# A fused attention and maxout FFN kernel: batch 0 split at query 240, and FFN block 0 in two token parts

## The chip, the cores and the metric

The kernel runs on one core of a Trainium2 chip. The core has five engines that each work through their own instructions in the order in which these were emitted: TensorE (PE in the profile, with PEld for its weight loads), VectorE (DVE), ScalarE (ACT), GpSimd (POOL) and SyncE (SP, which here only issues transfers). Transfers are issued from a queue on SP, ACT or POOL and run beside the engines. Only TensorE multiplies matrices, and its results land in PSUM, eight banks of 2 KB a partition, from where VectorE or ScalarE must fetch them.

The metric is the device time of one execution in microseconds (us), as a median over runs. A stamp such as 29.68 is a time from the start of the profiled span.

## The reference

Eight batches of eight-head attention with 16 "beacon" keys ahead of the 576 causal ones, and behind it, over all 4,608 tokens, an FFN that takes the maximum of three products and multiplies it once more:

```python
k_all = concatenate([beacon_k, k], axis=2)          # 16 + 576 keys
v_all = concatenate([beacon_v, v], axis=2)
scores = scale * q @ k_all.T                        # 8 batches, 8 heads, 576 queries, D = 64
scores = where(causal, -1e9, scores)                # beacon keys are seen by all queries
a = exp(scores - scores.max(-1))
a /= a.sum(-1) + 1e-9
x = (a @ v_all) as [4608 tokens, 512]               # token = batch * 576 + query
h = maximum(maximum(x @ w1, x @ w2), x @ w3)        # 768 columns
out = h @ w_out                                     # [4608, 512], fp32
```

## The kernel before, in words

**Quads.** The kernel goes through 16 "quads" Q = 2b + g: batch b, and four of its eight heads (g = 0 or 1). For each quad q and k lie transposed in SBUF (`qTs`, `kTs`, two buffers each, so quad Q takes the buffer of Q − 2). They come by a transfer, a cast to bf16 (done by an engine for quads 0 and 1, in the transfer itself for later ones, `load_qk16`), and four transposes on VectorE (`turn`, L180 to L188: k in two pieces, q in two).

**Scores in bursts.** Keys lie in five tiles t of up to 128; tile t is seen by the queries from `q_min[t]` = 0, 112, 240, 368, 496 on. The list `bursts` (L61) says which tiles with which queries are scored together; four bursts (c = 0 to 3) make a quad. `emit_scores` (L241) does the matmuls of a burst into two PSUM tiles `sc` of two heads each. There are only two such tiles, so a burst's scores wait for the exponentials of the burst before. For quads 0 and 1 the matmuls go two heads at a time, for the others four. `emit_exp(i)` (L267, ScalarE) turns one `sc` tile into `at_sb`; `emit_masks` (L284, GpSimd) sets to zero what lies beyond the diagonal.

**PV passes.** `pv_pass(Q, hf, part)` (L297) treats one half of the queries (hf = 0 or 1, 288 each). Part 0 multiplies `at_sb` with ones: the sums of the softmax, of which ScalarE makes reciprocals with a Ln and an Exp (L325, L327). Parts 1 and 2 multiply with V, and VectorE multiplies the result with the reciprocals into `xT` (L331), the transposed input of the FFN. PSUM has two tiles for these passes. `pv_pairs` puts the six passes of a quad in three pairs.

**The FFN.** Tokens go in nine blocks of 512. `mm1_unit(tb, ft, i)` makes 128 of the 768 columns of `x @ w_i` for one block: four matmuls of 512 tokens (two groups of 256 in block 4, where the ring of `xT` ends), and then a copy to `hT` for i = 0 (ScalarE, VectorE in block 0) or a maximum on VectorE for i = 1, 2. `mm2_unit` multiplies 128 tokens with `w_out`. A block is 18 + 4 = 22 units; PSUM has two tiles for them. Block 0 holds tokens of batch 0 alone, block 1 of batches 0 and 1, and so on.

**The order.** All is emitted by hand. `emit_all` (L493) goes through Q and c; a step emits a PV pair of the quad before, the burst's scores, one exponential, perhaps an FFN unit, the other exponential, the masks, and what `plan` holds for the step (loads, casts, transposes). FFN units are emitted up to a running limit `allowed`, which grows by `rate` a step, and only if the block's last batch is `ready`; `ready` goes to b − 1 at (4, 0) and then at step c = 3 of each even quad. Block 0 begins after quad 1's last PV pair, within step (2, 0), in an order by weights: six units of w1, then six of w2, six of w3. Rates are 22/11 = 2 units a step up to (4, 2) and 126/45 = 2.8 after it.

**Loads.** `begin` (L442) issues on SP's queue k and q of quads 0 and 1, the beacon keys of quad 1 (`load_first_beacon_k`), V of batch 0 in five tiles (`load_v`, cast to bf16 by VectorE), and the beacon keys of batch 1. POOL's queue then issues quad 2 at (0, 1), w1 at (0, 3), w2 at (1, 0), quad 3 at (1, 1), V of batch 1 from (1, 2) on, w3 at (2, 1), and w_out at (3, 0). In the text W0, W1 and W2 are the weights of i = 0, 1 and 2.

Of the kernel before, what the change touches and what calls it, by code (L numbers as in the profile page):

```python
# [16 lines left out]
def kernel(  # L17
# [43 lines left out]
    bursts = [  # L61
        [(0, 0, HALF), (3, q_min[3], S)],
        [(1, q_min[1], S)],
        [(2, q_min[2], S)],
        [(0, HALF, S), (4, q_min[4], S)],
    ]
    NC = len(bursts)
    at_piece = {}
    burst_at = []
    pos = 0  # L70
    for burst in bursts:
        start = pos
        for t, q0, q1 in burst:
            at_piece.setdefault(t, []).append((q0, q1, pos))
            pos += q1 - q0
        burst_at.append((start, pos))
    AT_W = pos
# [15 lines left out]
    nrm_pool = ctx.enter_context(tc.tile_pool(name="nrm", bufs=2))  # L93
    ffn_h = ctx.enter_context(tc.tile_pool(name="ffn_h", bufs=2))
# [97 lines left out]
    def load_v(b, queue=None):  # L192
        queue = queue or nc.sync
# [3 lines left out]
        for t in range(n_kt):  # L197
# [43 lines left out]
    def emit_scores(Q, c):  # L241
# [5 lines left out]
        a0, a1 = burst_at[c]  # L247

        for heads in ((0, 1), (2, 3)) if Q < n_quad else (range(HG),):
            off = 0  # L250
            for t, q0, q1 in bursts[c]:
# [24 lines left out]
    def emit_masks(Q, c):  # L276
        at_sb = at[Q]
        off = burst_at[c][0]
        for t, q0, q1 in bursts[c]:
# [17 lines left out]
    def pv_pass(Q, hf, part):  # L297
        b, g = divmod(Q, n_quad)
        at_sb, v_sb = at[Q], v_tiles[b]
        h0, h1 = hf * HALF, (hf + 1) * HALF  # L300
        runs = []
        for t in range(n_kt):
            for q0, q1, a in at_piece[t]:
# [3 lines left out]
        ps = pv_psum.tile([128, HALF], FP32, name="pv")  # L307
# [15 lines left out]
        if part == 0:  # L323
            lnd = nrm_pool.tile([128, HALF], FP32, name="lnd")
            nc.scalar.activation(out=lnd, in_=ps, func=AF.Ln)  # L325
            recip = nrm_pool.tile([128, HALF], FP32, name="recip")
            nc.scalar.activation(out=recip, in_=lnd, func=AF.Exp, scale=-1.0)  # L327
            recips[Q, hf] = recip
        else:
            c0 = b % RING * S + h0  # L330
            nc.vector.tensor_mul(xT[:, 2 * g + part - 1, c0 : c0 + HALF], ps, recips[Q, hf])  # L331
# [15 lines left out]
    def mm1_unit(tb, ft, i, pool, name):  # L347
# [15 lines left out]
        if i == 0 and tb > 0:  # L363
            nc.scalar.copy(hT[:, ft, :], ps)  # L364
        elif i == 0:

            nc.vector.tensor_copy(hT[:, ft, :], ps)
        else:
            nc.vector.tensor_max(hT[:, ft, :], hT[:, ft, :], ps)  # L369

# [35 lines left out]

    units = []
    for tb in range(n_tokb):
        last_b = (TOKB * (tb + 1) - 1) // S

        order = [(ft, i) for ft in range(n_ft) for i in range(3)]
        if tb == 0:
            order.sort(key=lambda x: x[1])
        for ft, i in order:
            units.append((last_b, mm1_unit, (tb, ft, i)))
# [15 lines left out]

    plan = {}
# [153 lines left out]
```

## Time and profile before

| | us |
|---|---|
| median of 3 runs | 295.66 (295.62 to 296.06) |
| profiled execution | 294.93 |
| its span, first to last instruction | 293.2 |
| TensorE busy in the span | 273.2 (93%) |
| ScalarE, VectorE, GpSimd busy | 159.2, 170.4, 87.9 |

The profile is one execution. A timeline row gives start, length, engine, line, operation, output and input, their shapes, a count of merged instructions (xN), and in brackets how long the engine stood idle before them and what released it. A row of the groups has busy time, mean ns of one, and idle time before. A busy TensorE is not TensorE at its full rate: the end of a matmul is modelled, and neighbours overlap.

### The profile page before, as it was taken

To read this page: it belongs to the slowest core of one execution; us is meant where nothing else is said; L and a number is where in the kernel's file an instruction comes from. 1 tells how busy PE (TensorE), PEld (TensorE's weight loads), DVE (VectorE), ACT (ScalarE), POOL (GpSimd) and SP (SyncE) were. 2 spreads that over 40 slices of the span, in tenths; PEclk is the share of its full clock that TensorE was granted. 3 is DMA by queue.
4 is the path that set the end of the run, shared out by engine and by line. 5 is a ranking of instruction groups with operands and counts; after the bars stand their busy time and mean duration, and the time that the engine had idled before them with its cause. 6 is when DMAs were issued, how large, how long until landed. Compare 5 with 4: busy or idle time off the path is not lost.

```text
span 293.2 us, 7619 instructions
## 1 busy us (share of the span) xinstructions
PE 273.2 (93%) x3208; PEld 137.1 (47%) x3246; DVE 170.4 (58%) x296; ACT 159.2 (54%) x246; POOL 87.9 (30%) x156
## 2 busy tenths in 40 slices
PE   0797999999999999999999999999989999999995
PEld 0245345434445444444548775544444445444442
DVE  3717769765656575647474656656653455555553
ACT  5798485468574655567645857465565742220210
POOL 0573953126231623134322623152212410000000
PEclk9999999999999999999999999999999999999999
DMA  7999999668147905491348506690038003003003
GB/s 251 231 183 206 121 187 185 111 188 147 36 83 202 189 2 81 144 218 35 49 141 186 101 2 116 192 167 2 23 133 155 2 2 132 14 0 134 13 0 143
DMA packets 51922, 33.05 MB, mean 113 GB/s; under 512 B 41264, under 2 KB 42288, under 8 KB 51888
## 3 DMA queue, kind: packets, MB, share of 16 engines
q1 hardware_dynamic: 41152, 20.40, 27.1%
q0 software_dynamic: 10464, 12.01, 26.0%
q8 instruction: 25, 0.41, 0.6%
q10 hardware_dynamic: 272, 0.15, 0.2%
q14 instruction: 9, 0.07, 0.1%
HBM read 35.13 MB, written 9.44 MB: 152 GB/s over the span
## 4 chain that ended last, share of the span: by engine, by line
PE 85%; ACT 7%; DVE 3%; issue 2%; DMA 1%; ACTq 0%; DVEq 0%
PE fps L356 41%; PE fps L376 14%; PE pv L315 12%; PE sc L256 10%; PE sc L356 5%; ACT at_sb L267 4%; DMA first<-in_beacon_k_dram 1%; PE sc L376 1%; DVE xT L331 1%; ACT lnd L325 1%; DVE qT L183 1%; DVE hT L369 1%; ACT recip L327 1%; ACT hT L364 1%; ACTq L141 0%
## 5 line engine op out<-in xcount | busy, mean ns | idle before, releaser
L356 PE MATMUL fps<-xT,w_sb 128*128 128x512 bf16 (+1 forms) x621 | 134.7, 355 | 2.8 <-issue 1.3
L267 ACT ACTIVATE at_sb<-sc 128x992 bf16<-128x992 f32 (+3 forms) x128 | 105.1, 860 | 55.0 <-PE sc L256 54.7
L369 DVE TENSOR_TENSOR hT<-hT,fps 128x512 bf16<-128x512 bf16 x96 | 65.8, 686 | 70.7 <-PE fps L356 62.4
L356 PEld LDWEIGHTS <-w_sb 128*128 128x128 bf16 x720 | 66.5, 98 | 72.0 <-issue 12.2
L284 POOL TENSOR_SCALAR_AFFINE_SELECT at_sb<-at_sb 128x512 bf16<-128x512 bf16 (+2 forms) x80 | 46.7, 593 | 135.5 <-ACT at_sb L267 128.3
L256 PE MATMUL sc<-qT,kT 32*128 32x288 bf16 (+4 forms) x768 | 43.1, 298 | 10.8 <-DVE qT L183 8.5
L364 ACT CAST hT<-fps 128x512 bf16<-128x512 f32 x42 | 24.6, 586 | 39.7 <-PE fps L356 39.7
L376 PE MATMUL fps<-w_out_sb,hT 128*128 128x512 bf16 x183 | 44.0, 379 | 0.7 <-issue 0.3
L331 DVE TENSOR_TENSOR xT<-pv,recip 128x288 bf16<-128x288 f32 x64 | 27.1, 450 | 10.8 <-PE pv L315 10.6
L384 DVE COPY y<-fps 128x512 f32<-128x512 f32 x32 | 22.1, 691 | 18.7 <-PE fps L376 14.9
L376 PEld LDWEIGHTS <-hT 128*128 128x128 bf16 x210 | 19.6, 97 | 26.4 <-issue 3.9
L256 PEld LDWEIGHTS <-kT 32*128 32x128 bf16 x768 | 17.4, 95 | 30.1 <-issue 16.2
L315 PE MATMUL pv<-at_sb,v_sb 128*32 128x288 bf16 (+4 forms) x1024 | 29.2, 255 | 1.7 <-DVE xT L331 1.6
L315 PEld LDWEIGHTS <-v_sb 128*32 128x32 bf16 (+1 forms) x1024 | 21.9, 96 | 15.4 <-issue 12.9
L183 DVE STREAM_TRANSPOSE kT<-c 128x256 uint32<-128x256 uint32 (+1 forms) x32 | 21.6, 705 | 3.6 <-ACT c L176 3.5
L183 DVE STREAM_TRANSPOSE qT<-c 128x256 uint32<-128x256 uint32 (+1 forms) x32 | 21.6, 705 | 0.0
L325 ACT ACTIVATE lnd<-pv 128x288 f32<-128x288 f32 x32 | 12.9, 402 | 13.8 <-PE pv L315 13.8
L356 PE MATMUL sc<-xT,w_sb 128*128 128x512 bf16 x70 | 18.2, 379 | 0.1
L209 POOL CAST v_sb<-vst 128x1024 bf16<-128x1024 f32 (+1 forms) x18 | 16.1, 893 | 6.8 <-DMA vst<-in_v_dram 6.8
L315 PE MATMUL pv<-at_sb,ones 128*32 128x288 bf16 (+4 forms) x512 | 15.2, 261 | 0.6 <-DVE xT L331 0.6
L327 ACT ACTIVATE recip<-lnd 128x288 f32<-128x288 f32 x32 | 14.2, 443 | 1.0
L315 PEld LDWEIGHTS <-ones 128*32 128x32 bf16 (+1 forms) x512 | 10.6, 97 | 8.2 <-issue 5.6
(35 smaller groups left out, 63.5 us busy)
## 6 DMA issues: line engine op xcount, KB each, us to landing
out_dram<-y SPq DMA_DIRECT2D x35, 256.0 KB, 2.0
vst<-in_v_dram SPq DMA_DIRECT2D x21, 256.0 KB, 4.7
c<-in_k_dram POOLq DMA_DIRECT2D x14, 288.0 KB, 4.4
c<-in_q_dram POOLq DMA_DIRECT2D x14, 288.0 KB, 5.2
w_sb<-in_moe_w_dram POOLq DMA_DIRECT2D x3, 768.0 KB, 9.2
vst<-in_v_dram SPq DMA_DIRECT2D x7, 224.0 KB, 3.5
vst<-in_v_dram SPq DMA_DIRECT2D x7, 160.0 KB, 5.3
w_out_sb<-in_moe_w_out_dram POOLq DMA_DIRECT2D x1, 768.0 KB, 11.2
```

What stands on the lines that cost most here:

```text
L183: nc.vector.transpose(dst.rearrange("p (t s) -> p s t", s=RUN)[:, s0:s1], src.rearrange("p (s d) -> p s d", d=DP),)
L256: nc.tensor.matmul(sc[h // 2][:, h % 2, off : off + w], kT[hs, 128 * t : 128 * (t + 1), j], qT[hs, q0:q1, j], start=(j == 0), stop=(j == 1 ...
L267: nc.scalar.activation(out=at_sb[:, 2 * i : 2 * i + 2, a0:a1], in_=sc[i][:, :, 0 : a1 - a0], func=AF.Exp, scale=scale,)
L284: nc.gpsimd.affine_select(out=view, in_=view, compare_op=ALU.is_ge, fill=0.0, base=q0 - (128 * t - Nb), pattern=[[0, HG], [1, edge - q0]], ...
L315: nc.tensor.matmul(ps[32 * j : 32 * j + 32, lo - h0 : hi - h0], lhsT, at_sb[0:n, j, a : a + hi - lo], start=(i == 0), stop=(i == len(runs) ...
L327: nc.scalar.activation(out=recip, in_=lnd, func=AF.Exp, scale=-1.0)
L331: nc.vector.tensor_mul(xT[:, 2 * g + part - 1, c0 : c0 + HALF], ps, recips[Q, hf])
L356: nc.tensor.matmul(ps[:, o0 : o0 + n], w_in[i][:, ct, 128 * ft : 128 * (ft + 1)], xT[:, ct, x0 : x0 + n], start=(ct == 0), stop=(ct == n_c ...
L364: nc.scalar.copy(hT[:, ft, :], ps)
L369: nc.vector.tensor_max(hT[:, ft, :], hT[:, ft, :], ps)
L376: nc.tensor.matmul(ps, hT[:, ft, 128 * tt : 128 * (tt + 1)], w_out_sb[:, ft, :], start=(ft == 0), stop=(ft == n_ft - 1),)
L384: nc.vector.tensor_copy(y, ps)
```

## The change

It does four things.

1. **Batch 0's queries are split at E = 240 instead of 288.** A class `Layout` now holds bursts and parts. Quads 0 and 1 use the layout `first`: its burst 0 holds all keys that queries 0 to 239 see, bursts 1 to 3 the rest (432 query columns each; burst 0 has 368). The other quads keep theirs.
2. **Order of batch 0** (`emit_first`, new): burst 0 and 1 of quad 0, burst 0 of quad 1, and then sums and products of the first parts of both quads, mixed with further bursts.
3. **FFN block 0 in two token parts, weight by weight** (`early_unit`, `block0`): for each w_i three units of two column tiles over tokens 0 to 239, then six units of one column tile over tokens 240 to 511; 27 units for 18, 144 matmuls for 72. For i = 0 VectorE copies the first part's results and ScalarE the second part's. Calls of `emit_block0` are put by hand between the bursts of quads 1 to 3. `emit_first` also holds all of quads 2 and 3 and of block 0. The loop of `emit_all` begins at quad 4, with `ready` = 1 and with 126/48 units a step.
4. **Loads**: the beacon keys of quad 1 go ahead of its q, those of batches 2 to 7 move into `begin`, SP loads only two tiles of batch 0's V and POOL the other three, W0 is issued before quad 2, and `load_w`, `load_quad`, `load_v16` stand in new places.

The PSUM tile of a PV pass becomes a full bank, and the reciprocals get a pool of four buffers.

```diff
+    E = q_min[2]
+    C1, C2 = E + 96, E + 192
+    first = Layout(
+        E,
+        [
+            [(1, q_min[1], E), (0, 0, E)],
+            [(0, E, S), (1, E, C1)],
+            [(1, C1, S), (2, E, C2)],
+            [(2, C2, S), (3, q_min[3], S), (4, q_min[4], S)],
+        ],
+    )
...
+    def layout(Q):
+        return first if Q < n_quad else usual
...
-        h0, h1 = hf * HALF, (hf + 1) * HALF
+        h0, h1 = layout(Q).parts[hf]
...
+    def early_unit(i, fts, x0, x1, copy):
+
+        if 0 not in hTs:
+            hTs[0] = ffn_h.tile([128, n_ft, TOKB], BF16, name="hT")
+        n = x1 - x0
+        bank = ffn_psum.tile([128, TOKB], FP32, name="fps")
+        ps = bank.rearrange("p (f n) -> p f n", f=len(fts))[:, :, 0:n]
+        for f, ft in enumerate(fts):
+            for ct in range(n_ct):
+                nc.tensor.matmul(
+                    ps[:, f],
+                    w_in[i][:, ct, 128 * ft : 128 * (ft + 1)],
+                    xT[:, ct, x0:x1],
+                    start=(ct == 0),
+                    stop=(ct == n_ct - 1),
+                )
+        hT = hTs[0][:, fts[0] : fts[-1] + 1, x0:x1]
+        if i == 0:
+            copy(hT, ps)
+        else:
+            nc.vector.tensor_max(hT, hT, ps)
...
+    block0 = []
+    for i in range(3):
+        for ft in range(0, n_ft, 2):
+            block0.append((early_unit, (i, (ft, ft + 1), 0, E, nc.vector.tensor_copy)))
+        for ft in range(n_ft):
+            block0.append((early_unit, (i, (ft,), E, TOKB, nc.scalar.copy)))
+    for tt in range(TOKB // 128):
+        block0.append((mm2_unit, (0, tt, ffn_psum, "fps")))
...
         load_qk(1, 1, (0, QS))
+        load_first_beacon_k(1, nc.sync)
         load_qk(1, 0, (0, QS))
-        load_first_beacon_k(1, nc.sync)
-        load_v(0)
+        load_v(0, 2)
         load_beacon_k(1, 2, nc.sync)
+        load_beacon_k(2, B, nc.sync)
...
+    def burst(Q, c, n=0):
+
+        emit_exp = emit_scores(Q, c)
+        emit_exp(0)
+        emit_block0(min(n, 1))
+        emit_exp(1)
+        emit_masks(Q, c)
+        emit_block0(max(n - 1, 0))
...
+        begin()
+        burst(0, 0)
+        load_w(0)
+        cast_v(0, 0, 2, by_dve)
+        burst(0, 1)
+        burst(1, 0)
+        load_v16(0, 2, 5)
+        sums(0, 0)
+        burst(0, 2)
+        load_quad(2)
+        sums(1, 0)
+        products(0, 0)
+        burst(0, 3)
+        load_w(1)
+        products(1, 0)
+        burst(1, 1, 2)
+        load_quad(3)
+        burst(1, 2, 1)
+        load_w(2)
+        sums(0, 1)
+        burst(1, 3)
+        turn_beacon_k(1, 2)
+        put_beacon_k(2, by_dve)
+        products(0, 1)
+        turn_all(2, 1)
+        turn_all(2, 0)
+        sums(1, 1)
+        burst(2, 0)
+        load_v16(1, 0, 2)
+        products(1, 1)
+        emit_block0(2)
+        burst(2, 1, 2)
+        load_v16(1, 2, 5)
+        burst(2, 2, 2)
+        put_beacon_k(3, by_pool)
+        load_w_out()
+        burst(2, 3)
+        load_quad(4)
+        for which in (1, 0):
+            emit_block0()
+            turn_all(3, which)
+        emit_block0()
+        turn_beacon_k(2, B)
+        burst(3, 0, 2)
+        emit_pv(pv_pairs(2)[0])
+        burst(3, 1, 2)
+        put_beacon_k(4, by_pool)
+        burst(3, 2, 2)
+        load_quad(5)
+        burst(3, 3, 2)
+        emit_block0(2)
+        emit_pv(pv_pairs(3)[0])
+        for Q in (2, 3):
+            for pair in pv_pairs(Q)[1:]:
+                emit_pv(pair)
+                emit_block0(min(2, len(block0) - 4))
+        turn_all(4, 1)
+        turn_all(4, 0)
+        while block0:
+            emit_block0()
...
-        early = range(n_quad * NC, (2 * n_quad + 1) * NC - 1)
-        early_rate = 22 / len(early)
-        rate = (len(units) - 3 * 22 - 6) / (NQ * NC - early.stop)
-        for Q in range(NQ):
+        rate = (len(units) - 2 * 22 - 6) / (NQ * NC - early_q * NC)
+        for Q in range(early_q, NQ):
```

More of the change, by code (lines that the diff above doesn't have):

```diff
@@ L277, in emit_masks @@
         at_sb = at[Q]
-        off = burst_at[c][0]
-        for t, q0, q1 in bursts[c]:
+        off = layout(Q).burst_at[c][0]
+        for t, q0, q1 in layout(Q).bursts[c]:
             edge = min(q1, 128 * t - Nb + k_rows[t])
```

166 lines of the change are left out of this document (78 added, 88 removed).

## The prediction

> **What bounds the kernel now.** I read the page first, then windows of engine busy time, then each engine's timeline over the first 60 us.
>
> ```profile
> span 293.2 us, 7619 instructions
> PE 273.2 (93%) x3208; PEld 137.1 (47%) x3246; DVE 170.4 (58%) x296; ACT 159.2 (54%) x246; POOL 87.9 (30%) x156
> PE   0797999999999999999999999999989999999995
> 8.00:28.00 20.00, 16.97 (x264) 8.19 (x264) 10.54 (x23) 16.70 (x25) 12.11 (x19) 1.00 1.07 205
> 36.00:44.00 8.00, 7.89 (x103) 3.65 (x108) 5.37 (x10) 6.18 (x10) 4.97 (x10) 1.00 1.12 185
> 44.00:52.00 8.00, 7.95 (x143) 4.14 (x140) 7.34 (x16) 4.61 (x9) 2.91 (x6) 1.00 1.05 175
> ```
>
> Each window row gives its stretch, its length, then busy us and instructions of PE, PEld, DVE, ACT and POOL, the granted clock, DMA share and GB/s. From 28 us on TensorE (PE) is full: 7.89 and 7.95 of 8 us. Whatever leaves it idle there is lost time. From 8 to 28 us ScalarE (ACT) sets the pace: 16.70 of 20. PE's 16.97 there are stretched matmuls, as the rows of the timelines show:
>
> ```profile
> 9.03 1.89 ACT L267 ACTIVATE at_sb<-sc 128x992 bf16<-128x992 f32 x2 [1.90 <-PE sc L256]
> 11.07 2.50 ACT L267 ACTIVATE at_sb<-sc 128x928 bf16<-128x928 f32 x3 [0.15 <-PE sc L256]
> 18.38 1.83 ACT L267 ACTIVATE at_sb<-sc 128x928 bf16<-128x928 f32 x2 [0.15 <-PE sc L256]
> 26.92 0.44 ACT L327 ACTIVATE recip<-lnd 128x288 f32<-128x288 f32 x1
> 21.35 0.92 PE L315 MATMUL pv<-at_sb,v_sb 128*32 128x288 bf16 x24
> 43.81 0.63 PE L315 MATMUL pv<-at_sb,v_sb 128*32 128x288 bf16 x24
> 46.71 1.18 PE L315 MATMUL pv<-at_sb,v_sb 128*32 128x288 bf16 x40
> 47.82 0.51 PE L256 MATMUL sc<-qT,kT 32*128 32x288 bf16 x16
> 40.63 0.90 PE L315 MATMUL pv<-at_sb,ones 128*32 128x288 bf16 x32
> 29.14 0.88 DVE L331 TENSOR_TENSOR xT<-pv,recip 128x288 bf16<-128x288 f32 x2 [0.48 <-PE pv L315]
> 29.68 1.67 PE L356 MATMUL fps<-xT,w_sb 128*128 128x512 bf16 x7 [0.16 <-issue]
> ```
>
> Exps follow each other with 0.15 us between them; batch 0's last reciprocal ends at 27.36 and the FFN starts at 29.68. The same 24 matmuls take 0.92 us at 21 us and 0.63 at 44: PE runs at about half speed until some 22 us, though the granted clock column says 1.00. So before 28 us PE has some 9 us of work, by its full-speed prices, in 20; it is this slack that the change can use.
>
> **The price list.** Exp, Ln, copy, multiply, transpose, mask and load:
>
> ```profile
> L267 ACT ACTIVATE at_sb<-sc 128x992 bf16<-128x992 f32 x10 | 9.4, 994 | 6.2 <-PE sc L256 6.1
> L267 ACT ACTIVATE at_sb<-sc 128x928 bf16<-128x928 f32 x10 | 9.0, 940 | 4.2 <-PE sc L256 4.2
> L267 ACT ACTIVATE at_sb<-sc 128x736 bf16<-128x736 f32 x8 | 5.9, 782 | 3.3 <-PE sc L256 3.2
> L267 ACT ACTIVATE at_sb<-sc 128x672 bf16<-128x672 f32 x8 | 5.5, 726 | 1.1 <-PE sc L256 1.1
> L325 ACT ACTIVATE lnd<-pv 128x288 f32<-128x288 f32 x8 | 3.2, 402 | 2.2 <-PE pv L315 2.2
> L364 ACT CAST hT<-fps 128x512 bf16<-128x512 f32 x8 | 4.7, 586 | 5.0 <-PE fps L356 5.0
> 34.35 1.24 DVE L183 STREAM_TRANSPOSE kT<-c 128x256 uint32<-128x256 uint32 x2
> 37.78 1.27 DVE L369 TENSOR_TENSOR hT<-hT,fps 128x512 bf16<-128x512 bf16 x2
> 29.47 1.17 POOL L284 TENSOR_SCALAR_AFFINE_SELECT at_sb<-at_sb 128x448 bf16<-128x448 bf16 x2 [3.94 <-ACT at_sb L267]
> 16.83 0.72 POOL L232 DMA_DIRECT2D w_sb<-in_moe_w_dram  x1
> w_sb<-in_moe_w_dram POOLq DMA_DIRECT2D x1, 768.0 KB, 8.3
> 24.20 0.84 POOL L225 DMA_DIRECT2D v_sb<-in_v_dram  x1
> 10.64 1.14 POOL L176 CAST c<-st 128x1152 bf16<-128x1152 f32 x1 [9.60 <-DMA st<-in_q_dram]
> 11.56 0.27 DVE L144 CAST first<-first 128x64 bf16<-128x64 f32 x1 [0.85 <-DMA first<-in_beacon_k_dram]
> 4.97 1.74 SPq L141 DMA_DIRECT2D first<-in_beacon_k_dram  x4
> ```
>
> Neighbours on ACT overlap by 0.1 us or so (two of 992 take 1.89), and a timeline row of PE includes 0.07 that overlaps with the next. The change's new widths lie between rows: a pair of exps of 864 (432 queries, two heads) costs 1.55, of 736 1.35 start to start; Ln and reciprocal together 0.6 for 240 queries, 0.75 for 336; an FFN copy of 272 columns 0.33; a max of 480 columns 0.6. Exp elements in all are unchanged (1,664 query columns per head either way). Half-speed scores of 432 queries take 0.74 per two heads, at full speed 0.42.
>
> **Halved FFN matmuls.** These rows stand for the split at 240:
>
> ```profile
> 129.57 2.84 PE L356 MATMUL fps<-xT,w_sb 128*128 128x512 bf16 x12
> 132.34 0.90 PE L315 MATMUL pv<-at_sb,ones 128*32 128x288 bf16 x32
> 160.91 2.86 PE L356 MATMUL fps<-xT,w_sb 128*128 128x256 bf16 x24
> 163.70 0.90 PE L315 MATMUL pv<-at_sb,ones 128*32 128x288 bf16 x32
> ```
>
> Three units as 12 matmuls of 512 take 132.34 − 129.57 = 2.77 us, as 24 of 256 take 2.79. So 72 more matmuls in block 0 cost 6 × 0.02 = 0.1 us. The sums and products of batch 0 get 24 more short matmuls (9 runs of four for 8, times 6 passes): the 24 matmuls of the 0.63 row are 0.023 apiece, columns included, so 24 more without more columns are 0 to 0.5 us; I take 0.2, since the columns are most of that price. Together **+0.3**. The Trainium skill (TensorEngine Tiling, Instruction Overhead) gives each matmul about 60 cycles of overhead. Added 72 times, at the 2.4 GHz of its page on TensorE, that would be 1.8 us, an estimate; the two pairs of rows don't agree with it, and they decide.
>
> **Batch 0, walked through ACT's order.** Stamps are sums of the rows above. Exps (0,0) 8.8 to 10.1, (0,1) 10.5 to 12.1. Next in order is now Q1's first burst. Its q is cast on POOL from 10.64 and turned on VectorE (DVE): 11.78 + 1.24 = 13.0. Before, DVE sat on the beacon rows until 11.56; the change issues those ahead, so this wait goes, but q1's own load goes four issues (1.74 us of SP) later. I take 13.4 (between 13.0 if its queue hides that, 14.7 if not). Half the scores at half speed: exps (1,0) 14.3 to 15.6. ACT idle 2.2, which Q0's own bursts filled before. Then (0,2) 16.2 to 17.7, Ln and reciprocal to 18.3. The second product of Q0 shares a PSUM buffer with Q1's sum, so it waits for that Ln, and (0,3)'s scores stand behind it: (0,3) 19.35 to 20.9, idle 1.05. (1,1) 21.45 to 23.0, idle 0.55. W0 is now the first load on POOL's queue, issued at 13.2; with 8.3 to landing it is there at 21.5, hidden by (1,1)'s scores until 22.0; each us later costs a us. Three tiles of V move from SP's queue (and two casts from DVE) to POOL's: 2.5 us of issues (three of 0.84) at 17 to 19.5, behind which stand the masks of (0,2) and (0,3), done at 22.3 and wanted at 25.3, and Q2's loads, issued at 20.1; hidden, with 3 us to spare for the masks. The tiles must land by 27. Two units of the first part (0.83 each) run 22.0 to 23.65, with (1,2)'s scores behind them: exps 24.3 to 25.85, idle 1.3. Third unit, sum (0,1), its reciprocal to 26.95, exps (1,3) to 28.5; batch 1's beacon rows (0.8 us of DVE) lie beside this. Two masks, 1.17: 29.7; only now do the last rounds of sum (1,1) run, and the reciprocal ends at 30.95 instead of 27.36. Meanwhile DVE, after the products of (0,1) at 28.85, turns Q2's k and q: two times 1.2, to 31.25. PE has scores (2,0) ahead of products (1,1): 31.35, products to 33.1, last multiply 33.75, first second-part unit **33.9**. The same walk over the kernel before ends at 30.0, where the row has 29.68.
>
> So 4.2 later, with three of 27 units done ahead (2.6 us of PE): **+1.6**.
>
> **Q2's and Q3's bursts.** Before, each step had some two whole units and a PV pair, over 3 us of PE beside 1.3 to 1.9 us of exp. Now a step of (2,1) to (2,2) has two half units: PE 0.5 + 2 × 0.47 = 1.4; ACT 1.65 (or 1.25) + two copies 0.66 = 2.3 (1.9), since W0's second-part copies go to ACT. Scores wait for the exps one burst back: PE idles 1.4 and 1.0. At (2,3) three first-part units of W1 (2.5 us of PE) alternate on DVE with Q3's turns: 0.6 + 1.2 + 0.6 + 1.2 = 3.6 us, and (3,0) needs the last turn: idle 2.2. Then Q2's four Ln and reciprocal instructions lie on ACT: (3,1) 0.35, (3,2) 1.6, (3,3) 0.6. Sum **+7.2**. Of the moved loads, W1 (issued about 22.3) and Q3 (23) get 8.3 us and more, and are due at 40: hidden by a margin of 6; uncovered, they cost us for us. Behind (3,3) all is FFN and PV; a product waiting for an Ln costs 0.4, and the four y copies stand behind Q4's turns (2.4 us): 1.1. **+1.5**. Changes between kinds of matmul, 0.16 us in the row of 29.68, cost nothing where PE waits anyway; four or five fall into these gaps: **−0.7**.
>
> **The steps after.** Q4 now starts with block 0 done, with 22 units of block 1 allowed at 126/48 = 2.625 a step. Block 2 becomes ready only at (6,3), 11 steps later: 28.9 allowed, 22 there. (6,1) and (6,2) go without FFN: PE has 0.83 + 0.42, then 0.56 + 0.31; ACT has a pair each of 1.76, 1.65, 1.25 and four Ln/reciprocal, 1.3. Idle 2.2. Block 2 runs out again before (8,3) (49.9 allowed, 44 there): 2.2. Before, the same point had 46.4 allowed for 44, less than one step without FFN, and PE is at 9 there on the page's line. **+4.4**. Opening block 1 stalls now thus:
>
> ```profile
> 62.47 0.59 ACT hT L364
> 63.06 0.64 ACT at_sb L267
> ```
>
> 1.3 us and a mode change, against 0.9 by the same sum at (4,1): **−0.5**.
>
> **Sum.** 0.3 + 1.6 + 7.2 + 1.5 − 0.7 + 4.4 − 0.5 = 13.8. The profiled execution took 294.93 (span 293.2 and 1.7 around it), 0.7 below the median of 295.66: 294.9 + 13.8 = **308.7 us**.
>
> **Rivals.** (1) *Faster*: three units really come out of idle time. If products (1,1) end by 32.3 (29.7 + 2.6) and the half units keep PE above 9.5 of 10 us through Q3, the start gains 2.6 and the opening stall 0.5, less 0.3: 292.1. For it speaks that PE has some 11 us to spare before 28 us; against it that 24 of 27 units need the second part anyway, and that exps and their masks stand between. 7%. (2) *The change does little of what it says*: three units of 27 move, (1) gains its 2.6, one starved stretch (2.2) takes it back, 294.5 to 296: 4%. (3) *Only the start and Q2/Q3 cost*, no starved steps: 304.3; for it, the catching-up steps could run ahead; against it, block 2 cannot start before (6,3). 17%. (4) *Loads or a slow PE*: W0 or Q2 late by 3 to 4 us, or half speed until 24 us (+1.5): 312 to 314; before, a load of Q3's k issued at 20.9 behind W1 took 9.4:
>
> ```profile
> c<-in_k_dram POOLq DMA_DIRECT2D x1, 288.0 KB, 9.4
> ```
>
> Against it, W0 has the queue to itself. 9%. (5) *PE falls back to half speed* in the thin stretch 34 to 53: its 13.7 us of work there would be 27.4 in 21 us, 6.5 more: 315. The rows show no fall-back after 23 us, but no such gaps either. 3%. The Trainium skill (TensorE: Matmul & The Clock Gate, Part 1) puts the fall-back behind an idle window of some 3.4 us; by that rule, with gaps of at most 2.2, (5) doesn't come.
>
> **How the numbers follow.** The forecast as summed has 60%, 306 to 311.
>
> Faster by over 0.2% (about what a measurement can tell) 0.07, within 0.04, slower 0.89. Range: 301 to 313, which leaves out (1), (2), (5) and half of (4), 18%; it takes in q1's two ends (13.0 to 14.7), the halved matmuls' and 2 us on each of the large terms.
>
> **What would show it.** The first FFN matmul at 22, the first of 272 columns at 34; ACT idle about 2 us near 12 to 14; PE near 6 of 10 from 34 to 53, with scores waiting for exps and once for a transpose of Q3; PE gaps near Q6 and Q8 with no FFN matmul between scores. PE dense from 22 us on would prove it wrong, above all a first 272-column matmul before 32.

## The result and the profile after

The changed kernel takes 320.26 us as a median of 4 runs (318.00 to 321.54), the kernel before 295.64 beside it (4 runs): a ratio of 1.083, 95% interval 1.076 to 1.090. The forecast was slower, 308.7 with a range of 301 to 313. The direction was right, the size was not: 13.8 us were expected, 24.6 came. Among the experiments below, one run each of a_y6, a_turn and a_order lay over 1.5% above its kernel's fastest; the ratios leave these three runs out, and without them the medians are 312.77, 317.29 and 318.66 us.

The profiled execution of the changed kernel took 318.0 us, so its span is to be held against the 293.2 us of before: 23.0 us more. Its page:

```profile
span 316.2 us, 7956 instructions
...
PE 283.9 (90%) x3390; PEld 150.1 (47%) x3390; DVE 168.9 (53%) x297; ACT 160.6 (51%) x252; POOL 89.7 (28%) x159
...
PE   0589868999999899959999799999999999999995
```

TensorE (PE) is 10.7 us busier than before, though the columns that it multiplies are the same: part of that is matmuls at half clock. The rest of the loss is idle time, and the third line shows where: the fifth to seventh slices of 7.9 us (32 to 55 us), and three dips in slices 14, 18 and 23 (from 103, 134 and 174 us on). The same in windows (length, then busy us and count of PE, PEld, DVE, ACT and POOL, granted clock, DMA share, GB/s):

```profile
34.00:44.00 10.00, 8.64 (x124) 5.70 (x117) 1.20 (x3) 8.10 (x14) 7.16 (x11) 0.89 0.88 88
44.00:48.00 4.00, 2.08 (x31) 1.50 (x30) 4.00 (x8) 0.35 (x1) 2.40 (x5) 1.00 1.33 121
48.00:58.00 10.00, 8.68 (x116) 5.96 (x113) 4.33 (x10) 7.85 (x12) 4.06 (x8) 1.00 0.73 122
100.00:108.00 8.00, 6.57 (x147) 3.63 (x148) 5.10 (x10) 6.39 (x10) 2.02 (x4) 1.00 0.99 205
135.00:147.00 12.00, 8.37 (x140) 4.64 (x139) 4.62 (x10) 6.22 (x11) 2.57 (x5) 0.86 0.89 204
172.00:178.00 6.00, 4.04 (x86) 2.21 (x78) 3.12 (x7) 3.99 (x7) 1.41 (x3) 1.00 0.48 167
```

Where before had 7.9 of 8 us from 36 us on, PE now has 19.40 of 24 in the first three rows. The last three rows lie in the loop, at bursts (6,1)–(6,2), (8,1)–(8,2) and (10,1)–(10,2): PE is 1.4, 3.6 and 2.0 us short in them.

**One point divides the loss.** The end of FFN block 0 is in both traces. Before it is the end of this row of PE's timeline, 61.06; by then bursts (4,0) and (4,1) had been scored, which the changed kernel does later, 0.56 and 0.53 us of PE:

```profile
54.52 0.62 PE L256 MATMUL sc<-qT,kT 32*128 32x288 bf16 x16
...
57.77 0.59 PE L256 MATMUL sc<-qT,kT 32*128 32x464 bf16 x8
58.30 2.76 PE L376 MATMUL fps<-w_out_sb,hT 128*128 128x512 bf16 x12
```

Less these, before is done with block 0 at 60.0. The rows of the changed kernel up to the same point:

```profile
22.59 3.38 PE L403 MATMUL fps<-xT,w_sb 128*128 128x240 bf16 x16
...
32.88 1.01 PE L282 MATMUL sc<-qT,kT 32*128 32x288 bf16 x16 [0.82 <-DVE qT L209]
...
36.11 1.42 PE L403 MATMUL fps<-xT,w_sb 128*128 128x272 bf16 x8
...
47.43 0.62 PE L282 MATMUL sc<-qT,kT 32*128 32x288 bf16 x16 [1.92 <-DVE qT L209]
...
69.46 2.75 PE L421 MATMUL fps<-w_out_sb,hT 128*128 128x512 bf16 x12 [0.63 <-DVE y L429]
```

Block 0 ends at 72.2, **12.2 us later**. The rest of the span is 244.0 us where before it was 233.2: **10.8 us** in the loop from quad 4 on. The prediction had 9.9 for the first part (0.3 + 1.6 + 7.2 + 1.5 − 0.7) and 3.9 for the second (4.4 − 0.5).

**In the loop** something stands in the rows that the prediction doesn't name. PE's timeline at the first two dips and in the third:

```profile
105.15 0.32 PE L282 MATMUL sc<-qT,kT 32*128 32x336 bf16 x2 [0.90 <-ACT at_sb L293]
105.98 0.47 PE L282 MATMUL sc<-qT,kT 32*128 32x336 bf16 x6 [0.51 <-ACT at_sb L293]
...
142.07 2.11 PE L341 MATMUL pv<-at_sb,v_sb 128*32 128x288 bf16 x40 [2.22 <-DVE xT L357]
...
176.94 1.18 PE L341 MATMUL pv<-at_sb,v_sb 128*32 128x288 bf16 x40 [1.76 <-DVE xT L357]
```

The waits for `at_sb` are the starved steps: scores without FFN between them wait for the exponentials. The waits of 2.22 and 1.76 us for `xT` are another thing, and VectorE's (DVE) timeline says which:

```profile
139.28 0.69 DVE L429 COPY y<-fps 128x512 f32<-128x512 f32 x1 [3.67 <-DMA out_dram<-y]
...
174.75 0.69 DVE L429 COPY y<-fps 128x512 f32<-128x512 f32 x1 [2.39 <-DMA out_dram<-y]
```

The fourth copy of an FFN block's output waits for a store to free one of the three `y` buffers. Behind it on VectorE stand the next quad's transposes and the multiplies into `xT`, and PE waits for those. The store that has to land first was issued at 131.82, right behind a quad's k and q, and took 7.3 us. VectorE's waits for such stores, total, times and longest:

```profile
DVE y L429 <- DMA out_dram<-y: 6.1, 2, 3.7
```

### The profile page after: what moved, and what is told of

Same layout as the page of the kernel before. It is cut to its first block, busy times and chain, and to the rows that moved or that the text cites. A ratio compares the mean times of both kernels' runs of the same rounds, so it can differ in the third digit from the quotient of the medians.

```text
span 316.2 us, 7956 instructions
## 1 busy us (share of the span) xinstructions
PE 283.9 (90%) x3390; PEld 150.1 (47%) x3390; DVE 168.9 (53%) x297; ACT 160.6 (51%) x252; POOL 89.7 (28%) x159
## 4 chain that ended last, share of the span: by engine, by line
PE 77%; ACT 9%; DVE 7%; DMA 4%; issue 2%; POOL 0%; SPq 0%; DVEq 0%
PE fps L382 35%; PE pv L341 11%; PE fps L421 11%; PE sc L282 9%; ACT at_sb L293 6%; PE sc L382 5%; PE fps L403 4%; DVE qT L209 3%; DMA out_dram<-y 2%; DVE kT L209 2%; ACT lnd L351 1%; DVE xT L357 1%; PE sc L421 1%; DMA st<-in_k_dram 1%; DMA first<-in_beacon_k_dram 1%
## 5 line engine op out<-in xcount | busy, mean ns | idle before, releaser
L293 ACT ACTIVATE at_sb<-sc 128x736 bf16<-128x736 f32 (+4 forms) x128 | 105.1, 860 | 68.0 <-PE sc L282 67.7
L382 PE MATMUL fps<-xT,w_sb 128*128 128x512 bf16 (+1 forms) x576 | 120.7, 353 | 0.0
L392 DVE TENSOR_TENSOR hT<-hT,fps 128x512 bf16<-128x512 bf16 x84 | 57.7, 687 | 67.7 <-PE fps L382 59.3
L282 PE MATMUL sc<-qT,kT 32*128 32x288 bf16 (+8 forms) x816 | 44.7, 294 | 20.9 <-DVE qT L209 13.2
L390 ACT CAST hT<-fps 128x512 bf16<-128x512 f32 x42 | 24.6, 585 | 48.8 <-PE fps L382 48.8
L341 PE MATMUL pv<-at_sb,v_sb 128*32 128x288 bf16 (+8 forms) x1040 | 32.2, 267 | 5.9 <-DVE xT L357 5.5
L357 DVE TENSOR_TENSOR xT<-pv,recip 128x288 bf16<-128x288 f32 (+2 forms) x64 | 27.6, 452 | 17.9 <-PE pv L341 16.3
L403 PE MATMUL fps<-xT,w_sb 128*128 128x240 bf16 (+1 forms) x144 | 19.9, 289 | 0.1
L351 ACT ACTIVATE lnd<-pv 128x288 f32<-128x288 f32 (+2 forms) x32 | 12.9, 403 | 10.8 <-PE pv L341 10.8
L341 PE MATMUL pv<-at_sb,ones 128*32 128x288 bf16 (+7 forms) x520 | 15.7, 255 | 1.1 <-POOL at_sb L310 1.0
L414 DVE TENSOR_TENSOR hT<-hT,fps 128x272 bf16<-128x272 bf16 (+1 forms) x18 | 9.1, 508 | 13.2 <-PE fps L403 10.7
```

Source lines behind the costliest of these rows:

```text
L282: nc.tensor.matmul(sc[h // 2][:, h % 2, off : off + w], kT[hs, 128 * t : 128 * (t + 1), j], qT[hs, q0:q1, j], start=(j == 0), stop=(j == 1 ...
L293: nc.scalar.activation(out=at_sb[:, 2 * i : 2 * i + 2, a0:a1], in_=sc[i][:, :, 0 : a1 - a0], func=AF.Exp, scale=scale,)
L341: nc.tensor.matmul(ps[32 * j : 32 * j + 32, lo - h0 : hi - h0], lhsT, at_sb[0:n, j, a : a + hi - lo], start=(i == 0), stop=(i == len(runs) ...
L357: nc.vector.tensor_mul(xT[:, 2 * g + part - 1, c0 : c0 + h1 - h0], ps, recips[Q, hf])
L382: nc.tensor.matmul(ps[:, o0 : o0 + n], w_in[i][:, ct, 128 * ft : 128 * (ft + 1)], xT[:, ct, x0 : x0 + n], start=(ct == 0), stop=(ct == n_c ...
L403: nc.tensor.matmul(ps[:, f], w_in[i][:, ct, 128 * ft : 128 * (ft + 1)], xT[:, ct, x0:x1], start=(ct == 0), stop=(ct == n_ct - 1),)
```

## The theories

*Theory.* A block that is ahead of its step runs out of units in one stretch of Q6, Q8 and Q10. The steps without FFN cost what the prediction said, about 2 us, and the block's four output units then fall together with the loads of a quad, so that their stores land late and the three `y` buffers don't suffice. The first 12.2 us are the thin half units of Q2 and Q3 and the walk of batch 0.

*Rivals.* The moved loads cost the time; 72 more matmuls cost it; TensorE's half clock costs it; the order of batch 0 (both quads' first parts first) costs it.

## Experiments on the loop

**a_pace** takes away the starved steps alone: units are allowed more slowly until block 2 is ready, and faster after.

```diff
-                allowed += rate
+                allowed += 2.0 if Q * NC + c < 27 else 104 / 37
```

> The changed kernel with another pace of the FFN units in the loop: 2 a step up to (6,2), then 104/37 = 2.81, so that block 1 lasts until block 2 becomes ready; as many units stay for the end. Of the 23.0 us by which the changed kernel's span is longer, 12.2 are there when block 0 ends and 10.8 come in the loop: 2.4 by (6,3), 5.5 more by (8,3), 2.8 more by (10,3). Theory (steps without FFN starve TensorE, and what hangs on them): nearly all of it goes, 8 to 11 us faster than the changed kernel, about 308 to 311. Rival (late stores of y hold VectorE whatever the pace): only the 2.2 and 2.2 of the two starved stretches go, 314 to 316.

It took 306.60 us (ratio to before 1.038, 1.035 to 1.040): 13.7 below the changed kernel by the medians. The span and the last output units of block 0 in PE's timeline:

```profile
core 0 of [0], span 304.7 us
...
68.65 2.75 PE L421 MATMUL fps<-w_out_sb,hT 128*128 128x512 bf16 x12 [0.63 <-DVE y L429]
```

From block 0's end (71.4) to the end of the span are 233.3 us, as before. VectorE waits for no store: the loads of the quad go out 7.8 us ahead of the block's first copy here (122.85 and 130.66). The whole loss of the loop, 10.7 us in the profiles, hung on one line of pacing.

**a_y6** leaves the starved steps and gives `y` six buffers.

```diff
-    ffn_y = ctx.enter_context(tc.tile_pool(name="ffn_y", bufs=3))
+    ffn_y = ctx.enter_context(tc.tile_pool(name="ffn_y", bufs=6))
```

> The changed kernel with six buffers for y instead of three, so that no copy of y waits for a store. VectorE waits 6.1 us for stores there, and TensorE behind it 2.2 us before (8,3), with half speed after it, and 1.8 us before (10,3). Theory (stores are a cause of their own): 4 to 6 us faster than the changed kernel. Rival (the starved steps lose this time anyway, TensorE would then wait for exponentials): 0 to 1 us.

313.14 us (310.94 to 315.99; ratio 1.056, 1.050 to 1.061), 7.1 below the changed kernel by the medians. In the profiles, where the loss can be placed, it is 4.5 us of the loop: block 0 ends at 72.1, the span at 311.6. The start of the last exponentials of quads 6, 8, 10 and 12 (ScalarE's timeline) gives the loss by stretch. Before:

```profile
93.42 0.78 ACT L267 ACTIVATE at_sb<-sc 128x736 bf16<-128x736 f32 x1 [1.62 <-PE sc L256]
...
124.57 0.78 ACT L267 ACTIVATE at_sb<-sc 128x736 bf16<-128x736 f32 x1 [1.62 <-PE sc L256]
...
155.86 0.78 ACT L267 ACTIVATE at_sb<-sc 128x736 bf16<-128x736 f32 x1 [0.59 <-PE sc L256]
...
187.18 0.78 ACT L267 ACTIVATE at_sb<-sc 128x736 bf16<-128x736 f32 x1 [0.59 <-PE sc L256]
```

After, and then with six buffers:

```profile
108.31 0.78 ACT L293 ACTIVATE at_sb<-sc 128x736 bf16<-128x736 f32 x1 [0.60 <-PE sc L282]
...
144.94 0.78 ACT L293 ACTIVATE at_sb<-sc 128x736 bf16<-128x736 f32 x1 [3.84 <-PE sc L282]
...
178.62 0.78 ACT L293 ACTIVATE at_sb<-sc 128x736 bf16<-128x736 f32 x1 [2.17 <-PE sc L282]
...
210.55 0.78 ACT L293 ACTIVATE at_sb<-sc 128x736 bf16<-128x736 f32 x1 [1.07 <-PE sc L282]
```

```profile
108.24 0.78 ACT L293 ACTIVATE at_sb<-sc 128x736 bf16<-128x736 f32 x1 [0.60 <-PE sc L282]
...
141.64 0.78 ACT L293 ACTIVATE at_sb<-sc 128x736 bf16<-128x736 f32 x1 [0.59 <-PE sc L282]
...
174.04 0.78 ACT L293 ACTIVATE at_sb<-sc 128x736 bf16<-128x736 f32 x1 [1.16 <-PE sc L282]
...
205.97 0.78 ACT L293 ACTIVATE at_sb<-sc 128x736 bf16<-128x736 f32 x1 [1.07 <-PE sc L282]
```

At Q6 the changed kernel is 14.9 us behind, 2.7 more than the 12.2 at block 0's end, and with six buffers likewise: no store is waited for there. From Q6 to Q8 the three kernels take 31.15, 36.63 and 33.40 us; from Q8 to Q10 31.29, 33.68 and 32.40; from Q10 to Q12 31.32, 31.93 and 31.93. So the second starved stretch costs 2.25 us without the wait for the store and 5.5 with it, the third 1.1 and 2.4; 0.6 follow, and 0.4 come back at the end.

**b_y6** gives the kernel before the same six buffers.

> The kernel before with six y buffers. Its trace has one wait of 2.1 us of VectorE for a store, and no wait of TensorE for VectorE of over 0.8 us. Theory (the wait is hidden): no difference that can be measured. Rival (what the changed kernel lost by it is lost here on a small scale): 0.5 to 1.5 us faster, and then faster than both kernels.

295.99 us (1.0015, 0.9998 to 1.0032): no difference. The profile of before puts one wait down to a store, and with six buffers the same copy waits as long, for PE. Before, and then with six buffers:

```profile
214.60 0.69 DVE L384 COPY y<-fps 128x512 f32<-128x512 f32 x1 [2.06 <-DMA out_dram<-y]
```

```profile
215.73 0.69 DVE L384 COPY y<-fps 128x512 f32<-128x512 f32 x1 [2.06 <-PE fps L376]
```

So the kernel before lost nothing to its three buffers. That the four copies of a block come in one row is not new either: from the first to the fourth they take 4.5 to 6.4 us before (210.56 to 215.90 in this block), and 4.5 in the changed kernel with six buffers (131.04 to 135.58). The buffers cost time only where the first store is still under way when the fourth copy comes.

## Experiments on Q2, Q3 and the start

**a_twice** gives the thin steps of Q2 and Q3 more half units, `burst(2, 1, 4)`, `(2, 2, 3)`, `(3, 0, 3)`, `(3, 1, 3)`, `(3, 2, 4)` for two each.

```diff
-        burst(2, 1, 2)
+        burst(2, 1, 4)
...
-        burst(2, 2, 2)
+        burst(2, 2, 3)
```

> The changed kernel with more half units beside each burst of quads 2 and 3 (four, three, three, three, four in place of two each), the work unchanged. TensorE idles about 7 us between the first 272-column unit and the last burst of quad 3. Theory (too little FFN beside each burst): 3 to 6 us faster than the changed kernel. Rival (ScalarE's exponentials and copies, and VectorE's transposes, set that stretch whatever TensorE does): less than 1 us.

317.14 us (1.075, 1.067 to 1.082), 3.1 less by the medians, though the intervals overlap. The scatter of the start falls out when the time is taken from the first 272-column unit to the end of block 0: 34.3 us (35.47 to 69.78) for the changed kernel's 36.1 (36.11 to 72.21), which a_pace and a_y6 have too. That is 1.8 us, less than the theory had and more than the rival.

**a_turn** puts Q3's transposes behind (2,1) and (2,2), where VectorE has room, and the three units of W1 together.

```diff
-        for which in (1, 0):
-            emit_block0()
-            turn_all(3, which)
-        emit_block0()
+        emit_block0(3)
```

(with `turn_all(3, 1)` after `burst(2, 1)` and `turn_all(3, 0)` after `burst(2, 2)`)

> The changed kernel with quad 3's transposes two bursts earlier, where VectorE stands idle, instead of between the maxima of W1's first part. Theory (scores (3,0) wait 1.9 us for the last transpose): 1.5 to 2.5 us faster than the changed kernel. Rival (the exponentials of (2,2) and (2,3) end no earlier, the gap moves on): 0 to 0.5 us.

318.05 us (1.074, 1.069 to 1.080), 2.2 less by the medians, with intervals that overlap; the same stretch takes 34.6 us (35.98 to 70.55), 1.5 less, and the wait of 1.92 us ahead of (3,0) is gone.

**a_order** scores (0,2) ahead of (1,0), so that ScalarE (ACT) has work while Q1's queries come.

```diff
         burst(0, 1)
+        burst(0, 2)
         burst(1, 0)
         load_v16(0, 2, 5)
         sums(0, 0)
-        burst(0, 2)
```

> The changed kernel with burst (0,2) ahead of burst (1,0), so that ScalarE has work while quad 1's q arrives. Theory of my walk (ScalarE idles 1.2 us there in the trace, but masks and quad 2's transposes end later in any case): 0 to 0.5 us faster than the changed kernel. Rival (batch 0 is one chain of exponentials, each idle us of ScalarE is paid): 1.0 to 2 us faster.

320.03 us (1.079, 1.071 to 1.086): no gain that can be told. In its profile the first 272-column unit comes 26.7 us behind the first exponentials (9.63 and 36.35), in the changed kernel 26.2.

**a_turn2** puts Q2's transposes on VectorE ahead of the multiplies of `products(0, 1)`.

```diff
-        products(0, 1)
         turn_all(2, 1)
         turn_all(2, 0)
+        products(0, 1)
```

> The changed kernel with quad 2's transposes ahead of the multiplies of (0,1) on VectorE. In the trace scores (2,0) wait 0.8 us for the last of them, and the clock falls at about that time. Theory: that wait goes, 0.8 us, and with less idle time TensorE may keep its clock, 0.8 to 2 us faster than the changed kernel. Rival (quad 2's loads land late, the transposes then hold up the multiplies): 0, or slower by up to 1 us.

319.43 us (1.082, 1.076 to 1.087): no gain that can be told.

**a_warm** puts eight matmuls that nobody reads in front of (2,0), to fill the stretch at 31 to 33 us after which the clock falls.

```diff
+        spare = ffn_psum.tile([128, TOKB], FP32, name="fps")
+        for x in (0, E):
+            for ct in range(n_ct):
+                nc.tensor.matmul(
+                    spare[:, x : x + E],
+                    w_in[0][:, ct, 0:128],
+                    xT[:, ct, 0:E],
+                    start=(ct == 0),
+                    stop=(ct == n_ct - 1),
+                )
         burst(2, 0)
```

> The changed kernel with eight spare matmuls of 240 columns between the sum (1,1) and quad 2's first scores, where TensorE waits 0.8 us for a transpose; their result is not read. In the changed kernel the granted clock falls to 0.50 from about 33 to 36 us, and scores (2,0) take 1.01 us for 0.62, the 56 matmuls behind them 2.35 for 1.31, the first eight of 272 columns 1.42 for 1.10. Theory (the fall-back comes of the thin stretch 30 to 33 us, and costs some 1.7 us): the clock stays at 1.0 or falls later, 0.5 to 1.7 us faster than the changed kernel, most of it by 38 us. Rival (the clock falls for the load of the microseconds before, as a window over more than 3 us sees it): no gain, or up to 0.5 us slower.

319.03 us (1.077, 1.072 to 1.082): no gain that can be told. Its windows, and above them those of the changed kernel:

```profile
30.90:32.90 2.00, 0.57 (x14) 0.31 (x14) 1.93 (x4) 0.76 (x2) 0.89 (x2) 0.96 1.11 212
33.00:36.00 3.00, 3.00 (x72) 2.10 (x67) 0.51 (x1) 1.96 (x3) 0.00 (x0) 0.50 1.04 205
47.00:51.00 4.00, 3.57 (x68) 2.29 (x69) 2.28 (x6) 2.83 (x5) 0.84 (x2) 1.00 1.14 184
```

```profile
33.00:36.00 3.00, 2.84 (x72) 1.86 (x72) 1.00 (x2) 2.38 (x4) 0.84 (x2) 1.00 0.97 193
46.00:50.00 4.00, 4.00 (x64) 2.20 (x52) 1.60 (x5) 2.88 (x5) 1.16 (x2) 0.57 1.14 188
```

The spare matmuls kept the clock at 1.00 at 33 to 36 us, and it fell in the next thin place instead, behind the wait for Q3's transposes: 0.57 from 46 to 50, where the changed kernel has 1.00. Measured from the first exponentials, (3,0) comes 0.8 us earlier than in the changed kernel, and (4,0) 0.1 later. a_turn2 shows the same exchange (1.00 from 30 to 38 us, 0.83 from 44 to 54). So one fall of the clock is worth about 0.8 us, an estimate from one pair of profiles, and filling one thin place moved it to another.

**b_halves** splits the kernel before's block 0 at 240 tokens and changes nothing else.

```diff
-        for x0, o0, n in ((c0, 0, n0), (0, n0, TOKB - n0)):
+        parts = ((c0, 0, n0), (0, n0, TOKB - n0))
+        if tb == 0:
+            parts = ((0, 0, 240), (240, 240, TOKB - 240))
+        for x0, o0, n in parts:
```

> The kernel before, with block 0's FFN matmuls of 512 tokens made as 240 and 272 into the same PSUM tile (144 for 72), and nothing else changed. My term: 0.1 us, no difference that can be measured. The Trainium skill (TensorEngine Tiling, Instruction Overhead), with 60 cycles for each matmul, would give an estimate of 1.8 us slower.

296.17 us (1.0011, 0.9990 to 1.0033): no difference, as the term of 0.1 us had it. The Trainium skill's 60 cycles for each matmul (TensorEngine Tiling, Instruction Overhead), an estimate of 1.8 us here, lies outside the interval, which ends at 1.0 us.

**b_loads** gives the kernel before a part of the new order of loads: the beacon keys of quad 1 ahead of its q, those of batches 2 to 7 in `begin`, W0 ahead of quad 2.

> The kernel before with a part of the change's loads alone: the beacon keys of quad 1 ahead of its q, those of batches 2 to 7 in begin, W0 ahead of quad 2. Theory (none of them lies on the path, quad 2 then lands some 3 to 5 us later, near 23 to 24 us, when its transposes begin at 23.6): 0 to 1 us slower. Rival (the change's loads delay the start, first scores at 7.7 to 9.1 us in it and at 8.0 before): 1 to 2 us slower.

295.83 us (1.0018, 1.0001 to 1.0034): up to 1 us. These loads cost next to nothing there, nowhere near the 24.6 us. The move of three tiles of V to POOL's queue is not in this run, and no other run tests it.

## Together, and what stays

**c_all** joins a_pace, a_y6, a_twice and a_turn.

> The changed kernel with four edits together: the pace of the loop (2, then 104/37), six y buffers, more half units beside each burst of quads 2 and 3, quad 3's transposes two bursts earlier. Theory (the loop's loss and the loss beside quads 2 and 3 are separate and add): 306.6 less 3.1 and 2.2, about 301; the six buffers add nothing once the pace is right; some 5 us stay, which batch 0 itself loses. Rival (they share the same idle time): 304 to 306.

303.38 us (1.026, 1.024 to 1.029): 3.2 under a_pace, less than the 5.3 of a_twice and a_turn by themselves. From the first 272-column unit to block 0's end it takes 32.3 us (36.51 to 68.81), 3.8 under a_pace's 36.1 (35.30 to 71.40): there the 1.8 and the 1.5 add up. But that unit starts 1.2 us later than in a_pace, behind a wait of 3.64 us for quad 1's scores where a_pace has 1.70. From block 0's end on it takes 233.2 us, as before; what is left over before, 8.8 us in the profiles and 7.8 by the medians, all lies ahead of that point.

**c_late** is c_all with another change: it moves three first-part units of W0 from (1,1) and (1,2), behind which (1,2)'s scores stand, to places behind (1,3): two after `products(0, 1)`, one after `sums(1, 1)`.

```diff
-        burst(1, 1, 2)
+        burst(1, 1)
...
-        burst(1, 2, 1)
+        burst(1, 2)
...
         products(0, 1)
+        emit_block0(2)
         turn_all(2, 1)
         turn_all(2, 0)
         sums(1, 1)
+        emit_block0(1)
```

> As the kernel with the four edits, and the three first-part units of W0 moved behind the products of (0,1), two of them, and behind the sum (1,1), one. In the changed kernel ScalarE idles 2.9 us before the exponentials (1,2) while TensorE runs two of these units at half speed ahead of their scores. Theory A (ScalarE's chain through batch 0 sets its end): 2 to 3 us faster than with four edits. Theory B, my walk (quad 2's transposes on VectorE end little earlier): 0.5 to 1.2 us faster. Either way slower than the kernel before.

302.74 us (1.025, 1.021 to 1.029), 0.6 under c_all, which can't be told from nothing. ScalarE's wait of 2.9 us ahead of (1,2) is gone, and another took its place on PE, since the transposes of Q2 now stand behind the units' copies on VectorE:

```profile
35.90 0.62 PE L282 MATMUL sc<-qT,kT 32*128 32x288 bf16 x16 [1.39 <-DVE qT L209]
```

**d_q1** is c_all with quad 1's q loaded ahead of its beacon keys again.

```diff
-        load_first_beacon_k(1, nc.sync)
         load_qk(1, 0, (0, QS))
+        load_first_beacon_k(1, nc.sync)
```

> c_all with quad 1's q loaded ahead of quad 1's beacon keys, as before the change. Theory A (what remains in c_all is ACT's wait for quad 1's scores, 3.64 us in its profile, and that wait comes from the load of q behind four more small loads): the wait falls to about 2 us, the time to 301.5 to 302.5. Theory B (the arrival of q varies from one execution to the next by more than the order moves it, and what remains is the order of batch 0's work itself): 302.7 to 304, the wait anywhere from 1.2 to 4 us.

302.79 us, with runs from 300.67 to 304.48 (1.023, 1.018 to 1.029). By the median nothing is told. The wait fell further than either theory had it, in c_all's timeline of ScalarE and then in d_q1's:

```profile
16.37 1.46 ACT L293 ACTIVATE at_sb<-sc 128x736 bf16<-128x736 f32 x2 [3.64 <-PE sc L282]
```

```profile
13.66 1.46 ACT L293 ACTIVATE at_sb<-sc 128x736 bf16<-128x736 f32 x2 [0.90 <-PE sc L282]
```

With equal first exponentials (9.28 and 9.31) quad 1 starts 2.7 us earlier, and the span ends 1.2 earlier (300.8 and 302.0). But the changed kernel itself, with the loads in c_all's order, has it at 14.52 with 1.17 of waiting, so that one profile of each doesn't show how much is the order and how much the scatter of the loads.

**d_quads** is d_q1 with quad 0's four bursts first, then quad 1's, in the same division at 240.

> d_q1 with batch 0's two quads scored one after the other, in the same division at 240: all four bursts of quad 0, then all four of quad 1, sums and products behind them; three units of the block's first part still ahead of Q2. Theory A' (scoring both quads' first part first is what costs: ACT waits once for quad 1's late queries, and again before (1,2) and (1,3)): ACT has quad 0's four bursts to do while quad 1's queries arrive, and 1 to 3 us are gained on d_q1, 299 to 301.5. Theory B' (the chain behind the last burst, sums, reciprocal, products, Q2's turns, sets the end of batch 0 in either order): within 0.7 us of d_q1.

304.67 us (1.031, 1.025 to 1.036), 1.9 above d_q1 by the medians, with intervals that overlap: theory A' falls, and B' was rather too low. ScalarE works from 9.5 to 22.5 us with no gap over 0.6, and then waits 3.61, 2.43 and 2.57 us for (1,2), for the last sum and for (2,0): the PV passes of both quads have gathered there. So scoring the quads one after the other wins nothing back, and neither did a_order: no run shows the changed order as part of the loss.

**d_mix** is c_late with q's load as in d_q1 and Q2's transposes ahead of `products(0, 1)`.

> c_late (three units of the block's first part moved behind the last burst of batch 0) with quad 1's q loaded ahead of quad 1's beacon keys and Q2's turns ahead of products(0,1), so that the scores of Q2 no longer wait for VectorE (1.39 us in c_late). Theory A: 1 to 2.5 us below c_late, 300.3 to 301.7. Theory B: within 0.7 us of c_late, 302 to 303.4, since what is saved at the turns is given back at the products' multiplies, which stand on the same VectorE.

300.54 us (1.017, 1.013 to 1.020), 2.2 below c_late, as theory A had it; the wait of 1.39 is gone. How much of the gain is q's load and how much the transposes, this run doesn't part. Its span, block 0's last row, and a window over Q2 and Q3 beside that of before:

```profile
core 0 of [0], span 298.9 us
...
62.97 2.76 PE L421 MATMUL fps<-w_out_sb,hT 128*128 128x512 bf16 x12
```

```profile
34.00:53.00 19.00, 17.19 (x205) 11.79 (x204) 10.40 (x22) 13.37 (x23) 12.01 (x20) 1.00 1.09 131
```

```profile
34.00:53.00 19.00, 18.79 (x273) 9.15 (x272) 15.71 (x30) 12.36 (x20) 9.59 (x18) 1.00 1.15 171
```

Its loop takes 233.2 us, and block 0 ends at 65.7, still 5.7 after before's 60.0, of which 1.6 are in this window of Q2 and Q3. No version beats the kernel before, and these 5.7 us are not taken apart further.

## Why the prediction was wrong in size

By its own steps, in the profiles (the span is 23.0 us longer, for 13.8; the 9.2 between them are 2.2, 0.1 and 6.9 of the first three points):

1. **The walk through batch 0: +1.6 was 3.8.** The first 272-column unit came at 36.11 for 33.9. These rows are ScalarE's:

```profile
9.90 1.46 ACT L293 ACTIVATE at_sb<-sc 128x736 bf16<-128x736 f32 x2 [1.78 <-PE sc L282]
...
14.52 1.46 ACT L293 ACTIVATE at_sb<-sc 128x736 bf16<-128x736 f32 x2 [1.17 <-PE sc L282]
...
26.50 1.67 ACT L293 ACTIVATE at_sb<-sc 128x864 bf16<-128x864 f32 x2 [2.92 <-PE sc L282]
```

   The first exponentials start 1.1 us late; that is within the loads' scatter, below. From there (1,2) is another 1.1 late (26.50 for 24.3): the two units ahead of its scores took 3.38 us at half speed, not 1.65, so ScalarE idled 2.92 for 1.3. The prediction had half speed ending at 22 and put full speed on exactly the units that started there.
2. **Q2 and Q3: the sum was right, partly by luck.** From that unit to the end of block 0 the sum of steps gives 36.0 us (33.9 to 69.9) and the trace 36.1. Some of the forecast waits are there: 1.92 for Q3's transposes (2.2), 0.37 for a Ln (0.4), 0.63 behind the output copies (1.1). But ahead of the scores that wait for exponentials PE idles 0.80 and 0.41 in Q2 for 1.4 and 1.0, and 0.77 and 0.51 in Q3 for 2.55. In all PE is idle there for 5.6 us, where the terms (7.2, 1.5 and −0.7) make 8.0, and busy for 30.5, where the rows of before, less the work done elsewhere and with the halved matmuls' 0.3, give an estimate of 27.7 (31.1 − 1.1 − 2.6 + 0.3). The two errors cancel; what makes the rows longer is not taken apart, and no run shows the −0.7 by itself. a_twice (1.8) and a_turn (1.5) took parts of this stretch back.
3. **The starved steps and the opening: +3.9 was 10.8.** This is the step that failed: "Block 2 runs out again before (8,3) (49.9 allowed, 44 there): 2.2." As a price of steps without FFN it was right, 2.25 at Q8 with six buffers; up to Q6 it came to 2.7, the opening of block 1 included, for 2.2 − 0.5 = 1.7. It put the stores at nothing: block 2, ahead of its step, sends its four outputs right behind the loads of a quad, the first store takes 7.3 us, and the fourth copy waits 3.67 us for it, in front of Q9's transposes on VectorE: 5.5 for 2.2. And it stopped at Q8: by its own count 70.9 units are allowed at (10,3) and 66 are there, and Q10 starves a third time, 2.4 us, of which 1.1 without the store. Together 2.7 + 5.5 + 2.4 + 0.6 − 0.4 = 10.8. The trace of before gave no warning: its one wait put down to a store was a wait for PE (b_y6).
4. **Halved matmuls, loads:** as forecast, as far as b_halves and b_loads test them: the 72 matmuls, and the loads but for V's. No run tests the 0.2 us of the short matmuls in batch 0, nor the 2.6 us of PE that the three units done ahead were to gain.

Of the rivals, (3), no starved steps, is a_pace: it was priced 304.3 and measured 306.6; the 2.3 between them are about the walk's 2.2. Of rival (4) the slow PE came true, half speed past 22 us, at 1.1 us; the late loads didn't. Rival (5), the clock, came in a short form that it hadn't: 0.50 for 3 us, not half speed through 20 us, and worth about 0.8 by a_warm's profile.

The median is 2.3 us above the profiled run. The other runs show granted clocks of 0.982 to 0.984 where this one shows 0.989, so perhaps one more fall of the clock; without their traces this stays an argument.

## What to carry to other kernels

Where work is paced by a running limit, check after every shift of its start whether the limit runs past what is ready: here that cost 10.7 us of the loop, and one line of pacing took it back. Of output units that come at another time than before, look which loads their stores now meet, whether the buffers last that long, and what stands behind the waiting copy on its engine. A wait that the profile puts down to a store can belong to another engine: more buffers tell. Of units moved into a stretch where matmuls still run at half speed, count double.

## What the runs showed of the hardware

**The clock falls without a long pause.** In the changed kernel it fell to 0.50 for 33 to 36 us, after two us (30.9 to 32.9) in which PE was busy for 0.57; the longest gap ahead of it was 0.82 us. It fell again at 142, where 40 PV matmuls took 2.11 us for 1.18; with six `y` buffers, and so without the gap of 2.22 us ahead of them, the clock stays at 1.00 there. The length of one gap doesn't decide it: behind gaps of 1.92 us (at 47.43) and 1.76 us (at 176.94) the changed kernel kept 1.00. The Trainium skill (TensorE: Matmul & The Clock Gate, Part 1) names an idle window of some 3.4 us for the fall, by which the prediction let rival (5) not come; the same part also tells of a kernel whose many short idles made the clock swing, and these rows look more like that second kind.

**Stores land late beside loads.** In the window of 125 to 150 us four stores of `y` took 6.0 us from issue to landing (the median); they were issued from 131.82 on, right behind a quad's k and q (130.86 and 131.39). Before, ten stores from 60 to 130 us took 2.0 (the median): the first store of the same block, issued 4.9 us behind such loads (112.47 and 117.32), took 2.7, and two that were issued behind loads of V took 5.0 and 4.9. The rows of the DMA view, after for the first store alone, and before for the ten:

```profile
c<-in_q_dram POOLq DMA_DIRECT2D x1, 288.0 KB, 7.2
out_dram<-y SPq DMA_DIRECT2D x1, 256.0 KB, 7.3
```

```profile
out_dram<-y SPq DMA_DIRECT2D x10, 256.0 KB, 2.0
```

The Trainium skill (DMA: Bandwidth & Descriptors, Queues, rings and completion order) says that a transfer's completion lands only after every earlier write of the same DMA engine, across its queues; a store as slow as the load beside it agrees with it, but no run here separates that from plain sharing of the engines.

**Loads scatter by more than an edit is worth.** With the same first loads, the first exponentials of the changed kernel and its variants start between 8.57 and 9.90 us. By that spread of 1.3 us, a difference below about 1 us (an estimate) between two single profiles of this start says nothing; that is one reason why a_order, a_turn2, a_warm and d_q1 can't be ranked.
